# The out stage of the last three four-unit groups as seven block products, its halves placed in the next group's first step

## The chip, the cores and the metric

One core of one Trainium2 chip. The time is that of one execution on the device in microseconds (us); for the kernel before it is 228.29, the median of three runs (227.87 to 228.46). Engines: PE does matmuls (PEld is its weight loads), DVE, ACT and POOL work element by element, SP issues DMAs.

## The reference, cut to what matters

Attention with a decay, over blocks of 64 positions, and then a bilinear feed-forward layer on its output. The second part is what the change touches.

```
# q, k, v: (4, 8, 768, 64); per head, with powers of lam:
intra = (q_blk @ k_blk.T * Dmask) @ v_blk
out[blk] = intra + (q_blk * lam_pow) @ kv_state
kv_state = lam**64 * kv_state + (k_blk * rev_pow).T @ v_blk
# x = attention output, (3072, 512); w_a, w_b: (512, 1536); w_out: (1536, 512)
return ((x @ w_a) * (x @ w_b)) @ w_out
```

## The kernel before

The 3072 rows are 24 units of 128 positions, six for each batch entry. They go through the feed-forward layer in eight groups of 4, 1, 2, 4, 4, 4, 4 and 1 units (`GROUPS`, numbered from 0). While PE computes group g, the attention of later units is woven in: `PLAN[g]` lists (slot, piece, unit), and `hook(slot)` (L859) is called at fixed places of the group and emits the pieces of that slot. Nothing reorders them afterwards: each engine gets its instructions in the order in which the code emits them, PE, DVE, ACT, POOL and the DMA queue of SP alike. A piece of an early slot may so run far ahead of PE's place, if nothing ahead of it on its own engine waits.

Pieces: P scales k and q by powers of lam into `qk` (POOL, L318), makes `vb` of v, has SP transpose `qk` by DMA into `qkT` (L346), and asks for the loads of a unit two later (`pump`, L230). S is the scores (L374, 16 small matmuls) and their masks, a product with `lotri` on DVE (L391). V updates the running kv state (L438) and copies it (`KV_ENG` says by which engine). O forms the attention output of one or two units (L408) and ACT copies it into `xT` (L431). X forms three sums of `xT` for the next group on DVE (L620 to L622). C casts a part of w_out, WS forms one of eight sums of w_a and w_b (L206), W stores an early output.

Groups 3 to 6 (`Z_GROUPS`) run `ffn_z` (L625). Its first step computes x @ w_a and x @ w_b as seven products of blocks in place of eight (Strassen's way): six *pairs* n, each one chunk of 128 columns of both halves of d_ff. A product is four matmuls of 128x256. Of a pair, U (banks 0 and 1 in turn) takes products 1, 5, 3 and 2, V (banks 2 and 3 in turn) 4 and 6, W (bank 4) 0; ACT saves what stands in U and V in between (`snap`, L647: u1, v1, u2), DVE subtracts these from W (L679), U (L688) and V (L689). The last product 2 of a pair comes in the next pair (`finish`, L652): ACT copies U, and one DVE product makes `ab` of the pair's chunks (L658). Two slots a pair.

The second step, the *out stage* (L691 to L717), is plain: four tiles of 128 rows, each 12 matmuls of 128x512 with `ab` as weights and `wo_sb` streaming (L697), then an ACT copy (L552) and a store of 256 KB from SP's queue. Eight slots lie in it, and in it stand masks and X for the next group. Group 7 (one unit) runs `ffn` (L560): 12 times a and b of 128 columns with an ACT copy (L519) and a DVE product (L537), then 36 short matmuls (L557) and three copies and stores.

Eight 4 KB buffers (`wst`, L113) serve the weight loads, the snaps, `oab` and early outputs. Loads of q, k and v have four buffers each (L114); SP issues the four V loads of group 0 (L154) ahead of the first weight loads (L183).

Of the kernel before, what the change touches and what calls it, by code (L numbers as in the profile page):

```python
# [22 lines left out]
def _bc(ap, dims):  # L23
# [8 lines left out]
W_BUFS = 8  # L32
# [11 lines left out]
    0: [(0, 'V', 3), (8, 'C', 0), (9, 'C', 1), (15, 'C', 2), (18, 'C', 3), (23, 'PK', 4),  # L44
        (26, 'C', 4), (26, 'T', 4), (27, 'WS', 0), (28, 'WS', 1), (29, 'C', 5), (29, 'S', 4),
        (30, 'PV', 4), (31, 'WS', 2), (32, 'WS', 3), (33, 'O', 4), (34, 'WS', 4),
        (35, 'PK', 5), (35, 'PV', 5)],
    1: [(0, 'V', 4), (2, 'T', 5), (3, 'PK', 6), (4, 'WS', 5), (6, 'PV', 6), (6, 'S', 5),
        (7, 'T', 6), (8, 'WS', 6), (10, 'S', 6), (11, 'WS', 7), (12, 'O2', (5, 6)),
        (13, 'P', 7)],  # L50
    2: [(2, 'V', 6), (2, 'P', 8), (3, 'P', 9), (4, 'W', None), (5, 'V', 7), (5, 'PK', 10),
        (7, 'V', 8), (8, 'S', 7), (8, 'S', 8), (10, 'V', 9), (10, 'W', None), (11, 'PV', 10),
        (11, 'W', None), (12, 'P', 11), (12, 'W', None), (12, 'Q', (7, 8, 9, 10)),
        (13, 'P', 12), (14, 'O2', (9, 10)), (15, 'X', 3), (15, 'P', 13), (15, 'W', None)],
    3: [(0, 'S', 11), (2, 'P', 14), (4, 'S', 12), (7, 'S', 13), (7, 'P', 15),
        (9, 'O2', (11, 12)), (11, 'S', 14), (11, 'V', 13), (15, 'P', 16),
        (16, 'O2', (13, 14)), (16, 'X', 4), (17, 'P', 17), (17, 'P', 18), (17, 'S', 15),
        (19, 'S', 16), (19, 'P', 19)],
    4: [(3, 'V', 11), (3, 'V', 15), (4, 'S', 17), (5, 'O2', (15, 16)), (6, 'S', 18),
        (7, 'P', 20), (8, 'O2', (17, 18)), (9, 'V', 17), (9, 'P', 21), (11, 'S', 19),  # L60
        (13, 'S', 20), (14, 'X', 5), (19, 'V', 19), (19, 'P', 22)],
    5: [(4, 'S', 22), (5, 'S', 21), (8, 'O2', (19, 20)), (10, 'V', 21), (11, 'O2', (21, 22)),
        (11, 'P', 23), (16, 'X', 6)],
    6: [(0, 'S', 23), (11, 'O', 23)],
}
Z_GROUPS = (3, 4, 5, 6)
KV_ENG = dict(enumerate(["dve"] * 10 +
                        ["act"] * 2 +
                        ["dve"] +
                        ["act"] * 3 +  # L70
                        ["dve"] * 6 +
                        ["act"] +
                        ["dve"]))
VB_ENG = dict(enumerate(["pool"] * 7 +
                        ["dve"] * 3 +
                        ["act"] * 2 +
                        ["dve"] +
                        ["pool"] * 4 +
                        ["dve"] +
                        ["pool"] * 2 +  # L80
                        ["act"] +
                        ["dve"] +
                        ["pool"] * 2))
# [3 lines left out]
def kernel(  # L87
# [25 lines left out]
    wst_pool = ctx.enter_context(tc.tile_pool(name="wst", bufs=W_BUFS))  # L113
    ld_pool = ctx.enter_context(tc.tile_pool(name="ld", bufs=4))  # L114
    prep_pool = ctx.enter_context(tc.tile_pool(name="prep", bufs=6))
# [3 lines left out]
    a_pool = ctx.enter_context(tc.tile_pool(name="a", bufs=4))  # L119
# [5 lines left out]
    sum_pool = ctx.enter_context(tc.tile_pool(name="sum", bufs=1))  # L125
    ctx.enter_context(tc.manual_schedule())
# [36 lines left out]
    staged = {}  # L163
    w_off = [sum(W_CHUNKS[:i]) for i in range(len(W_CHUNKS) + 1)]
# [7 lines left out]
    def load_w(kind, c):  # L172
        t = wst_pool.tile([128, 1024], F32, name="wst", tag="wst")
        if kind == "o":
            t = t[:].rearrange("p (k n) -> p k n", k=2)
            nc.sync.dma_start(out=t, in_=wo_r[:, 2 * c:2 * c + 2, :])
        else:
            w = W_CHUNKS[c]
            t = t[:, :KS * w].rearrange("p (k n) -> p k n", k=KS)
            r = wa_r if kind == "a" else wb_r  # L180
            if c in W_HALVES:
                t = t.rearrange("p k n -> p (k n)").rearrange("p (k n) -> p k n", k=2)
            nc.sync.dma_start(out=t, in_=w_part(r, c))  # L183
        staged[kind, c] = t

    def cast_w(kind, c, eng):
        t = staged.pop((kind, c))
# [4 lines left out]
        if eng == "act":  # L192
            nc.scalar.copy(dst, t)
        elif eng == "first":
            nc.vector.tensor_copy(dst[:, :3, :128], t[:, :3, :128])
            nc.gpsimd.tensor_copy(dst[:, 3:, :128], t[:, 3:, :128])
            nc.gpsimd.tensor_copy(dst[:, :, 128:], t[:, :, 128:])
        else:
            nc.vector.tensor_copy(dst, t)  # L199
# [3 lines left out]
    wz = {kind: sum_pool.tile([128, 4, 2, HF], BF16, name="wz_" + kind, tag="wz_" + kind)  # L203
          for kind in "ab"}

    def weight_sum(i):  # L206
        kind, j = "ab"[i % 2], i // 2
        w, z = (wa_sb if kind == "a" else wb_sb), wz[kind]
        a11, a12 = w[:, 0:2, :HF], w[:, 2:4, :HF]
        a21, a22 = w[:, 0:2, HF:], w[:, 2:4, HF:]  # L210
        if j == 0:
            nc.vector.tensor_sub(z[:, 0], a22, a21)
        elif j == 1:
            nc.vector.tensor_sub(z[:, 1], a11, z[:, 0])
        elif j == 2:
            nc.vector.tensor_sub(z[:, 2], a12, z[:, 1])
        else:
            nc.vector.tensor_add(z[:, 3], a11, a21)
# [11 lines left out]
    def pump():  # L230
        while pending:
            kind, c = pending[0]
            if kind in "abo":
                if len(staged) >= W_BUFS:
# [9 lines left out]
    idle_sb = singles.tile([128, 512], BF16, name="idle_sb")  # L244
# [13 lines left out]
    for w, src in (("q", q), ("k", k)):  # L258
# [3 lines left out]
        for c in range(0, HP, n_c):  # L262
            t = wst_pool.tile([128, 1024], F32, name=w + "4", tag="wst")[:, :n_c * 512]
            t = t.rearrange("p (c b x) -> p c b x", c=n_c, b=2)
# [3 lines left out]
            staged[w + "4", c] = t  # L268
# [109 lines left out]
    def masks(u, kq):  # L378
        ms = mask(kq, split=False)
        U[u]["m"] = lambda i, hp: ms[i][:, hp, :]  # L380

    def mask(kq, split=False):
        ms = []
        for i in range(2):
            m = msk_pool.tile([128, HP, 128], BF16, name=f"m{i}", tag=f"m{i}")
            if split and i == 1:
# [97 lines left out]
    def pieces_O(us, nxt=()):  # L484
# [6 lines left out]
        for b in range(2):  # L491
            for u in us:
                intra(u, b)
            evac_o(us, b)
# [22 lines left out]
    def a_copy(ps, gt):  # L517
        a_sb = a_pool.tile([128, 512], BF16, name="a_sb", tag="a")
# [26 lines left out]
    def store(row, op, lo, hi, queue=None):  # L545
        if row < g_u0[KEEP_GROUPS]:
            o_sb = wst_pool.tile([128, 1024], F32, name="o_kept", tag="wst")[:, :d_model]
# [67 lines left out]
    def x_sums(g):  # L615
        xT = gx[g]
        z_add = sum_pool.tile([128, 2, 512], BF16, name="z_add", tag="z_add")
        z_sub = sum_pool.tile([128, KS, 256], BF16, name="z_sub", tag="z_sub")
        z_mix = sum_pool.tile([128, 2, 256], BF16, name="z_mix", tag="z_mix")
        nc.vector.tensor_sub(z_sub, xT[:, :, 0:256], xT[:, :, 256:512])  # L620
        nc.vector.tensor_add(z_add, xT[:, 0:2, :], xT[:, 2:4, :])
        nc.vector.tensor_add(z_mix, xT[:, 0:2, 0:256], xT[:, 2:4, 256:512])  # L622
        xz[g] = (z_add, z_sub, z_mix)

    def ffn_z(g, u0, xT, hook):  # L625
        z_add, z_sub, z_mix = xz.pop(g)
        ab = ab_pool.tile([128, FC, 512], BF16, name="ab", tag="ab")
        NP = FC // 2
# [16 lines left out]
        def snap(ps, tag):  # L645
            t = wst_pool.tile([128, 2, 256], F32, name=tag, tag="wst")
            nc.scalar.copy(t, ps)  # L647
            return t

        P = {}  # L650

        def finish(n):  # L652
            d = P.pop(n)
            product(d["U"], n, 2)
            oab = d["oab"]
            nc.scalar.copy(oab[:, 0], d["U"])  # L656
# [5 lines left out]
        def begin(n):  # L662
            d = P[n] = {}
            d["U"] = z_bank("U", n % 2)
            product(d["U"], n, 1, True)
            d["u1"] = snap(d["U"], "u1")

        for n in range(NP):
            if n != 1:
                begin(n)  # L670
            d = P[n]
            oab = d["oab"] = wst_pool.tile([128, 4, 2, 256], BF16, name="oab", tag="wst")
            d["V"] = z_bank("V", 2 + n % 2)
            product(d["V"], n, 4, True)
            v1 = snap(d["V"], "v1")
            hook(2 * n)
            W = z_bank("W", 4)
            product(W, n, 0, True)
            nc.vector.tensor_sub(oab[:, 2], W, d["u1"])  # L679
            product(d["U"], n, 5)  # L680
            u2 = snap(d["U"], "u2")
            if n:
                finish(n - 1)
            else:
                begin(1)
            product(d["V"], n, 6)
            product(d["U"], n, 3)
            nc.vector.tensor_sub(oab[:, 1], d["U"], v1)  # L688
            nc.vector.tensor_sub(oab[:, 3], d["V"], u2)  # L689
            hook(2 * n + 1)  # L690
# [4 lines left out]
        def out_part(t, fs):  # L695
# [7 lines left out]
        out_part(0, early[:3])  # L703
        finish(NP - 1)
        out_part(0, early[3:])
        hook(FC)
        out_part(1, early)
        hook(FC + 1)
        out_part(0, late)
        hook(FC + 2)  # L710
        out_part(1, late)
        hook(FC + 3)
        for t in (2, 3):
            out_part(t, early[:6])
            hook(FC + 2 * t)
            out_part(t, early[6:] + late)
            hook(FC + 2 * t + 1)  # L717
# [8 lines left out]
    scr = [ab_pool.tile([128, FC, 512], BF16, name="scratch", tag="ab") for _ in range(2)]  # L726
# [4 lines left out]
    def scale4(w, i, j):  # L731
# [5 lines left out]
        if w == "k" or j == 1:  # L737
            staged.pop((w + "4", c if w == "k" else 2 * i))
# [185 lines left out]
```

## Time and profile before

| | us |
|---|---|
| median of three runs | 228.29 (227.87 to 228.46) |
| the profiled execution | 228.72 |
| its span, first to last instruction | 227.0 |
| start, to b's first matmul in group 0 (L510) | 22.54 |
| group 4: pairs / out stage | 119.2 to 142.2 / to 153.0 |
| group 5: pairs / out stage | 153.0 to 174.4 / to 185.3 |
| group 6: pairs / out stage | 185.3 to 204.7 / to 215.6 |
| group 7 and the end | 215.6 to 227.0 |
| DVE / ACT / POOL busy | 154.6 / 117.0 / 59.2 |

How to read it: a row of the timeline has start, length, engine, line, operation, output<-inputs, sizes, count, and in brackets the idle time of that engine before it with what ended it. The length of one matmul holds its way through the array, so the pace of a stream is read from a run of equal ones, its length divided by their count. The chain of waits follows the end of the program back through whatever released each step; a piece has start, length and line. All times are us from the span's start unless ns is written.

### The profile page before, as it was taken

What the parts mean: (1) busy time and instruction counts of PE and PEld (TensorE: products, weight loads), DVE (VectorE), ACT (ScalarE), POOL (GpSimd) and SP (SyncE); (2) the same over time, 40 slices, a digit from 0 to 9 for tenths busy, and PEclk for the clock granted to TensorE, in tenths of its full rate; (3) what the DMA queues carried; (4) which work ended last, traced back from release to release, by engine and by line L of the source; (5) the groups of instructions that cost most, each with busy time, mean ns of one, the idle gap of its engine ahead of it and who ended that gap; (6) DMA issues with size and microseconds to landing.
All of it is one profiled execution on the core that took longest, in us unless ns stands there. A gap on an engine that the chain in (4) does not pass through costs nothing.

```text
span 227.0 us, 5349 instructions
## 1 busy us (share of the span) xinstructions
PE 217.8 (96%) x2127; PEld 148.3 (65%) x2127; DVE 154.6 (68%) x257; ACT 117.0 (52%) x233; POOL 59.2 (26%) x73
## 2 busy tenths in 40 slices
PE   7798999999899999999999999999999999999994
PEld 2374444447678758877458887448887458885493
DVE  0994773969959868999356988676988318773050
ACT  2685465037443267656247685127576236672261
POOL 6061000147843254424424434460000000000000
PEclk9999999999999999999999999999999999999999
DMA  4999999999999999999999999943020030000311
GB/s 131 318 261 350 359 387 319 271 222 196 233 192 200 240 187 269 212 233 184 181 247 237 205 186 231 169 153 92 3 48 1 27 144 18 1 3 0 141 46 46
DMA packets 97544, 39.40 MB, mean 174 GB/s; under 512 B 85488, under 2 KB 92016, under 8 KB 97520
## 3 DMA queue, kind: packets, MB, share of 16 engines
q1 hardware_dynamic: 97232, 39.00, 80.4%
q8 instruction: 16, 0.26, 0.5%
q10 hardware_dynamic: 288, 0.07, 0.1%
q14 instruction: 8, 0.07, 0.1%
HBM read 28.32 MB, written 6.29 MB: 152 GB/s over the span
## 4 chain that ended last, share of the span: by engine, by line
PE 77%; DMA 8%; SPq 6%; DVE 4%; issue 2%; ACT 1%; ACTq 0%; DVEq 0%
PE op L697 18%; PE U L641 15%; PE b_ps L510 9%; PE op L557 9%; PE a_ps L510 7%; PE V L641 7%; PE o_ps L408 4%; DMA wst<-in_moe_w_b_dram 4%; PE W L641 4%; SPq L154 3%; DMA qkT<-qk 3%; PE kq L374 2%; DMA q<-in_q_dram 2%; PE kvd L438 1%; SPq L183 1%
## 5 line engine op out<-in xcount | busy, mean ns | idle before, releaser
L697 PE MATMUL op<-wo_sb,ab 128*128 128x512 bf16 x192 | 43.3, 379 | 0.0
L391 DVE TENSOR_TENSOR m<-kq,lotri 128x512 bf16<-128x512 f32 x47 | 29.7, 681 | 13.7 <-PE kq L374 13.6
L647 ACT COPY u<-U 128x512 f32<-128x512 f32 x48 | 27.8, 587 | 18.7 <-PE U L641 17.9
L318 POOL TENSOR_TENSOR qk<-kf,lp_k 128x512 bf16<-128x512 f32 x18 | 19.7, 1096 | 53.2 <-DMA kf<-in_k_dram 51.0
L537 DVE TENSOR_TENSOR ab<-a_sb,b_ps 128x128 bf16<-128x128 bf16 (+2 forms) x48 | 19.3, 415 | 20.9 <-ACT a_sb L519 13.6
L697 PEld LDWEIGHTS <-ab 128*128 128x128 bf16 x192 | 18.2, 98 | 20.7
L318 POOL TENSOR_TENSOR qk<-qf,lp_q 128x512 bf16<-128x512 f32 x20 | 24.8, 1239 | 23.0 <-DMA qf<-in_q_dram 23.0
L510 PE MATMUL b_ps<-xT,wb_sb 128*128 128x128 bf16 (+2 forms) x192 | 27.6, 272 | 1.2 <-DVE wb_sb L199 1.0
L510 PE MATMUL a_ps<-xT,wa_sb 128*128 128x128 bf16 (+2 forms) x200 | 27.7, 268 | 0.0
L552 ACT COPY o_sb<-op 128x512 f32<-128x512 f32 (+2 forms) x21 | 11.1, 547 | 31.3 <-PE op L697 28.8
L658 DVE TENSOR_TENSOR ab<-oab 128x1024 bf16<-128x1024 bf16 x24 | 18.8, 783 | 9.1 <-ACT oab L656 9.0
L519 ACT CAST a_sb<-a_ps 128x128 bf16<-128x128 f32 (+2 forms) x48 | 17.2, 376 | 13.1 <-PE a_ps L510 11.5
L557 PE MATMUL op<-wo_sb,ab 128*128 128x512 bf16 (+2 forms) x120 | 22.5, 337 | 0.2 <-DVE ab L537 0.2
L510 PEld LDWEIGHTS <-wb_sb 128*128 128x128 bf16 x192 | 15.8, 98 | 7.7 <-DVE wb_sb L199 1.5
L641 PEld LDWEIGHTS <-wz_a 128*128 128x128 bf16 x192 | 18.3, 98 | 3.3 <-issue 0.3
L510 PEld LDWEIGHTS <-wa_sb 128*128 128x128 bf16 x200 | 16.0, 98 | 6.7 <-DVE wa_sb L199 0.4
L641 PEld LDWEIGHTS <-wz_b 128*128 128x128 bf16 x192 | 18.7, 97 | 2.2
L688 DVE TENSOR_TENSOR oab<-U,v 128x512 bf16<-128x512 f32 x24 | 16.4, 683 | 3.4 <-PE U L641 2.6
L641 PE MATMUL U<-xT,wz_a 128*128 128x256 bf16 x96 | 18.3, 272 | 0.0
L641 PE MATMUL U<-xT,wz_b 128*128 128x256 bf16 x96 | 18.3, 272 | 0.0
L679 DVE TENSOR_TENSOR oab<-W,u 128x512 bf16<-128x512 f32 x24 | 16.3, 681 | 0.9 <-PE W L641 0.9
L431 ACT CAST xT<-o_ps 128x512 bf16<-128x512 f32 (+1 forms) x24 | 12.2, 556 | 9.0 <-PE o_ps L408 8.9
(96 smaller groups left out, 337.0 us busy)
## 6 DMA issues: line engine op xcount, KB each, us to landing
vf<-in_v_dram SPq DMA_DIRECT2D x24, 256.0 KB, 5.0
qf<-in_q_dram SPq DMA_DIRECT2D x20, 256.0 KB, 5.1
kf<-in_k_dram SPq DMA_DIRECT2D x20, 256.0 KB, 5.4
out_dram<-o_sb SPq DMA_DIRECT2D x18, 256.0 KB, 2.2
wst<-in_moe_w_a_dram SPq DMA_DIRECT2D x6, 512.0 KB, 8.4
wst<-in_moe_w_b_dram SPq DMA_DIRECT2D x6, 512.0 KB, 9.0
wst<-in_moe_w_out_dram SPq DMA_DIRECT2D x6, 512.0 KB, 9.1
out_dram<-o_kept SPq DMA_DIRECT2D x5, 256.0 KB, 4.6
```

The costliest lines, as they stand in the source:

```text
L318: eng_of(eng).tensor_mul(dst.rearrange("p (c b) d -> p b c d", b=2), x[:].rearrange("p (b c) d -> p b c d", b=2), lp.rearrange("p (b c) o ...
L391: nc.vector.tensor_mul(m, kq[i], lotri_bc)
L510: nc.tensor.matmul(ps[:, lo:hi], lhsT=w_sb[:, s, f * 128:(f + 1) * 128], rhs=xT[:, s, lo:hi], start=(s == 0), stop=(s == KS - 1), skip_gro ...
L519: nc.scalar.copy(a_sb[:, :gt], ps[:, :gt])
L537: nc.vector.tensor_mul(ab[:, f, :gt], a_sb[:, :gt], ps[:, :gt])
L557: nc.tensor.matmul(op[:, lo:hi], lhsT=ab[:, f, t * 128:(t + 1) * 128], rhs=wo_sb[:, f, lo:hi], start=(f == 0), stop=(f == FC - 1))
L641: nc.tensor.matmul(ps[:, k, :], lhsT=wt[:, s, n * 128:(n + 1) * 128], rhs=rhs[i][:, s, :], start=(fresh and k == 0 and s == 0), stop=True, ...
L647: nc.scalar.copy(t, ps)
L658: nc.vector.tensor_mul(ab[:].rearrange("p (h i) (t c) -> p h i t c", h=2, t=2)[:, :, n], o5[:, :, :, 0, :], o5[:, :, :, 1, :])
L679: nc.vector.tensor_sub(oab[:, 2], W, d["u1"])
L688: nc.vector.tensor_sub(oab[:, 1], d["U"], v1)
L697: nc.tensor.matmul(ops[t][:].rearrange("p a b -> p (a b)"), lhsT=ab[:, f, t * 128:(t + 1) * 128], rhs=wo_sb[:, f, :], start=(f == 0), stop ...
```

## The change

The out stages of groups 4, 5 and 6 become seven products of blocks too: with ab split into four blocks (two halves of d_ff by two of 256 rows) and w_out into four (halves of d_ff by halves of its 512 columns). Three things are needed for it.

- Sums of w_out, once: five of 128x1536 (`out_sum`, piece WO, in group 3; POOL three, DVE two).
- Sums of ab for each of the three groups: eight of 128x768 (`ab_sum`, piece SM), 14 of the 24 on POOL, ten on DVE.
- The products as 14 *halves* (`out_half`, piece H), each six matmuls of 128x256 (three chunks, two row tiles). Two accumulators (banks 3 and 4); ACT saves three values and copies one out, DVE subtracts three; four stores of 256 KB, each of 256 columns of two row tiles.

The halves of group g are hooked into the pairs of group g+1 (those of group 6 between the 12 chunks of group 7). A pair has three slots now. In groups 5 and 6 ("joined") a pair has this order: U product 1, the last product of the pair before, slot 3n, V product 4, U product 5, slot 3n+1, V 6, U 3, slot 3n+2, W 0; V and W share bank 2. Groups 3 and 4 keep W in bank 4 and V in banks 2 and 3. Group 3 keeps the plain out stage.

With it the plan is drawn up anew. In group 4, P of 21 goes from slot 9 of the old two-slot pairs to slot 17, with 22, behind X of group 5, which POOL does, and an ab sum; P of 23 goes to slot 2 of group 5. S of 21, 22, 23 stand at slots 3, 6, 9 of group 5. Eleven masks go by an ACT copy (`raw_kq`) and a DVE product of it. Two WS, two C and three WO are POOL's. SBUF: the pool of eight is split into seven snaps of 2 KB, two `oab` and staging in tiles that are free early; q, k, v loads have three buffers each, `qk` and `vb` five.

```diff
+    4: [(0, 'V', 15), (1, 'S', 17), (2, 'P', 19), (4, 'O2', (15, 16)), (6, 'S', 18),
+        (9, 'P', 20), (10, 'O2', (17, 18)), (12, 'S', 19), (14, 'X', 5), (14, 'SM', (4, 0)),
+        (17, 'SM', (4, 2)), (17, 'S', 20), (17, 'SM', (4, 4)), (17, 'P', 21), (17, 'P', 22)],
+    5: [(0, 'SM', (4, 1)), (0, 'SM', (4, 3)), (1, 'H', (4, 0)), (1, 'V', 19),
+        (2, 'H', (4, 1)), (2, 'P', 23), (2, 'O2', (19, 20)), (3, 'S', 21), (4, 'H', (4, 2)),
...
-    ld_pool = ctx.enter_context(tc.tile_pool(name="ld", bufs=4))
-    prep_pool = ctx.enter_context(tc.tile_pool(name="prep", bufs=6))
+    ld_pool = ctx.enter_context(tc.tile_pool(name="ld", bufs=3))
+    prep_pool = ctx.enter_context(tc.tile_pool(name="prep", bufs=5))
...
+        p = (4, 0, 5, 6, 2)[i]
+        x, y = {4: (b11, b12), 0: (b11, b21), 5: (b11, b22), 6: (b12, b22), 2: (b21, b22)}[p]
+        eng = eng_of(WO_ENG[i])
+        (eng.tensor_sub if p in (2, 4) else eng.tensor_add)(wo_sums[p], x, y)
...
+            if i >= 2 - n_act:
+                raw_kq = raw_pool.tile([128, HP, 128], BF16, name="raw_kq", tag="raw")
+                nc.scalar.copy(raw_kq, kq[i])
+                nc.vector.tensor_mul(m, raw_kq, lotri_bc)
...
+            U = z_bank("U", pairs[0] % 2)
+            pairs[0] += 1
+            product(U, n, 1, True)
+            u1 = snap(U)
+            if joined:
+                if fin:
+                    fin.pop()()
+                hook(3 * n)
+            X = z_bank("V", 2 if joined else 2 + n % 2)
+            product(X, n, 4, True)
+            v1 = snap(X)
...
+            product(U, n, 5)
+            u2 = snap(U)
...
+            hook(3 * n + 1)
+            product(X, n, 6)
+            if joined:
+                nc.vector.tensor_sub(oab[:, 3], X, u2)
+            product(U, n, 3)
+            nc.vector.tensor_sub(oab[:, 1], U, v1)
...
+            hook(3 * n + 2)
+            if joined:
+                W = z_bank("W", 2)
+                product(W, n, 0, True)
+                nc.vector.tensor_sub(oab[:, 2], W, u1)
+            fin.append(lambda n=n, U=U, oab=oab: last_product(n, U, oab))
...
+    def ab_sum(g, i):
...
+        if j == 0:
+            eng.tensor_add(z3, a11, a21)
+        elif j == 1:
+            eng.tensor_sub(a21, a22, a21)
+        elif j == 2:
+            eng.tensor_sub(z1, a11, a21)
+        else:
+            eng.tensor_sub(z1, a12, z1)
...
+    O_ORDER = (4, 1, 5, 6, 3, 0, 2)
+
+    def out_half(g, i):
+        d = outs[g]
+        p, h = O_ORDER[i // 2], i % 2
...
+        c = "U" if p in (1, 5, 3, 2) else "V"
+        fresh = h == 0 and p in (4, 1, 0)
+        if fresh:
+            d[c] = z_bank("op", 3 if c == "U" else 4)
+        ps = d[c]
+        for n in range(h * NP // 2, (h + 1) * NP // 2):
+            for t in range(2):
+                nc.tensor.matmul(ps[:, t, :], lhsT=lhs[p][:, n, t * 128:(t + 1) * 128],
+                                 rhs=rhs[:, n, :], start=fresh, stop=True, skip_group_check=True)
+                fresh = False
+        if h:
+            if p in (4, 1, 5):
+                d[{4: "v1", 1: "u1", 5: "u2"}[p]] = snap(ps)
+            else:
+                o = o_pool.tile([128, 2, 256], F32, name="o_sb", tag="osb")
+                if p == 2:
+                    nc.scalar.copy(o, ps)
+                else:
+                    nc.vector.tensor_sub(o, ps, d[{6: "u2", 3: "v1", 0: "u1"}[p]])
...
+                nc.sync.dma_start(out=rows.rearrange("t p n -> p t n"), in_=o)
```

## The prediction

> **What bounds the kernel now.** First the page's busy shares, then the chain that ended last.
>
> ```profile
> PE 217.8 (96%) x2127; PEld 148.3 (65%) x2127; DVE 154.6 (68%) x257; ACT 117.0 (52%) x233; POOL 59.2 (26%) x73
> ...
> PE 77%; DMA 8%; SPq 6%; DVE 4%; issue 2%; ACT 1%; ACTq 0%; DVEq 0%
> PE op L697 18%; PE U L641 15%; PE b_ps L510 9%; PE op L557 9%; PE a_ps L510 7%; PE V L641 7%; PE o_ps L408 4%; DMA wst<-in_moe_w_b_dram 4%; PE W L641 4%; SPq L154 3%; DMA qkT<-qk 3%; PE kq L374 2%; DMA q<-in_q_dram 2%; PE kvd L438 1%; SPq L183 1%
> ```
>
> TensorE carries three quarters of the chain, and the largest single line is L697, the out stage that the change rewrites (192 matmuls, four groups). The stretches by stage say whether that stage is PE from end to end (columns: PE, weight loads, DVE, ACT, POOL busy, clock):
>
> ```profile
> 119.20:142.20 23.00, 22.78 (x267) 18.57 (x264) 19.82 (x32) 16.16 (x31) 10.21 (x11) 1.00 1.20 215
> 142.20:153.00 10.80, 10.78 (x61) 5.13 (x61) 7.39 (x9) 2.25 (x4) 5.64 (x6) 1.00 0.91 163
> 153.00:174.40 21.40, 21.40 (x269) 18.22 (x267) 17.91 (x29) 14.34 (x27) 0.00 (x0) 1.00 0.18 38
> 174.40:185.30 10.90, 10.90 (x56) 5.18 (x55) 2.94 (x6) 3.66 (x8) 0.00 (x0) 1.00 0.20 74
> ```
>
> These are the pairs of group 4, its out stage, the pairs of group 5, its out stage. PE is full at clock 1.00 in all; DVE is nearly as full beside the pairs and almost idle beside the out stages. So a PE microsecond removed is worth a microsecond, as long as what is put in its place does not wait.
>
> **The out stages.** Spacings come from the chain:
>
> ```profile
> 154.06 0.44 PE W L641 x4
> 154.50 0.87 PE U L641 x8
> ...
> 205.87 9.73 PE op L697 x45
> ```
>
> A 128x512 matmul takes 9.73/45 = 0.216 us, a 128x256 one 0.87/8 = 0.109. The old stage is 48 x 0.216 = 10.4 us; seven products of six chunks and two row tiles are 84 x 0.109 = 9.15. That is 1.23 us a group, **3.7 us** for three. The 84 weight loads are as many per column as in the pairs, which already run at that spacing, so they add nothing. The evictions (four ACT copies of 0.59 us a group) become four ACT copies and three DVE subtractions (0.68 each); four 256 KB stores stay four. All lie beside other PE work.
>
> **Sums.** Eight sums a group of 128x768 and five once of 128x1536. DVE's 128x1024 sum took 0.68 us undisturbed and its 128x1536 one 0.94, so 768 is about 0.52; POOL has only 512-element products (1.04, and 1.16 for the one mask), so I take 1.55 for 768, 2.05 for 1024 and 3.1 for 1536. Ten of the 24 go to DVE, 14 to POOL; three of the five weight sums, two old weight sums, two casts and all of group 5's x sums go to POOL too. DVE has 3.5 us free beside group 5's pairs and 5 beside group 6's, and the stages grow by 9 us each: the total fits, order decides.
>
> **Two engines on one memory.** While POOL scaled unit 21, DVE's product took twice its time:
>
> ```profile
> 137.25 1.05 POOL L318 TENSOR_TENSOR qk<-kf,lp_k 128x512 bf16<-128x512 f32 x1 [4.37 <-DMA kf<-in_k_dram]
> 137.48 1.35 DVE L658 TENSOR_TENSOR ab<-oab 128x1024 bf16<-128x1024 bf16 x1 [0.69 <-ACT oab L656]
> 138.25 1.49 POOL L318 TENSOR_TENSOR qk<-qf,lp_q 128x512 bf16<-128x512 f32 x1
> 138.76 0.68 DVE L688 TENSOR_TENSOR oab<-U,v 128x512 bf16<-128x512 f32 x1
> ```
>
> 1.35 for 0.68, then POOL's 1.49 for 1.04, a meeting costing each side some 0.45 to 0.67; the subtraction from PSUM kept its 0.68. I use these meetings.
>
> [...]
>
> **A joined pair (groups 5 and 6).** V and W share one bank now. With 0 at the end of the last W: U1 to 0.44, the last pair's U to 0.88, V to 1.31, U to 1.75, a half (6 x 0.109 = 0.65) to 2.4, V to 2.84, U to 3.28, a half to 3.93, W to 4.37. Three waits are tight. The next V waits for DVE's subtraction of W: 0.06 + 0.68 + 0.05 = 0.79 against 0.88, 0.09 of slack, gone when DVE takes a half's output just before. W waits for the subtraction of V, 2.9 to 3.6 against 3.93. DVE's product (ACT copy 1.0 to 1.6, product 1.65 to 2.3) must be done before that: a delay d puts W at 3.03 + d, so 0.9 costs nothing and 1.6 costs 0.7. Where units 19/20 and 21/22 put their O work, ACT is about 0.7 us behind and the next u1 costs some 0.1. I take 0.8 for the twelve pairs, from 0 to 3 (0.25 a pair).
>
> **Unit 21.** Its scaling moves from slot 9 of group 4 to slot 17, on POOL behind group 5's three x sums and one ab sum, and its scores stay early in group 5. Count from group 4's start (119.2 before). PE reaches the end of O(17,18)'s matmuls after 3.28 (pair 0: six products, V, S), 4.20 (seven and O), 3.50 (seven and S), five products 2.19 and 0.80: 14.0; ACT has xT at 15.1. POOL: 2.05 + 2.05 + 1.05, ab sum 1.55, to 21.8; two or three meetings with DVE make 22.9; two scales 2.1, so 25.0 (the load, asked for after unit 19, has landed by then: at 137.25 in this trace). Then SP's transpose: landing took 3.0 to 6.1, median 4.8, 3.9 for the two on an idle DMA. PE wants it at slot 3: group 4's pairs end at 22.1, group 5's first pair with two halves, V 19 and O(19,20) takes 5.7, two U products 0.88: 28.7. With 3.9 the wait is 0.3, with 4.8 it is 1.2; I take **0.7**, from 0 to 2.7 (4.8, two more meetings and 0.6 for slower sums). All of PE's list stands behind it. Units 22 and 23 leave POOL at 28 and, after 23's load, at 33.6, 1 to 3 us before their scores; later ab sums have about 1 us.
>
> DVE's third ab sum waits for that POOL sum (22.9) in front of group 4's last product and group 5's first subtractions; unit 20's masks hold DVE to 23.4 anyway. Beside the x sums, DVE's products of the last two pairs may be held up for most of 2.05 us; then the subtraction of U, which the next pair's last product waits for, is late: **0.4**, from 0 to 1.3.
>
> **The start.** The load tiles of q, k and v go from four buffers to three, so SP's fourth V load waits for POOL's cast of the first.
>
> ```profile
> 10.68 1.05 SPq L154
> 11.72 0.04 issue
> 11.77 1.14 SPq L183
> ```
>
> That cast ran 12.11 to 12.72, so this issue moves from 10.68 to 12.75 and the weight loads behind it by up to 1 us; b's first chunk, at 21.76, is what PE then waits for. DMA is full from 6 us on (share 0.97 or more in each 2 us), and the V loads ahead land until 14.5, so the queue should stay fed: **0.2**, from 0 to 1.0. It can't gain.
>
> **Groups 0 to 3.** Casts, weight sums and masks move between engines (eleven masks become an ACT copy and a DVE product of SBUF, 0.59 and 0.4 for 0.68), all beside a full PE. In group 1 PE now waits 0.49, 0.61 and 0.15 us on DVE (k scale, ab); two weight sums leave DVE there, but one of 3.1 us now sits on POOL ahead of unit 6's scales: 50.5 + 3.1, then two scales of 1.04, or 1.70 and 1.49 as here, to 55.7 or 56.8. T of unit 6 wants them at slot 5: 52.1 + 0.2 + six chunks of 0.45 + V + T = 55.7. So 1.25 becomes 0 to 1.1, or more if DVE's sums bunch: **-0.4**, from -1.2 to +0.9. The 0.32 for unit 13's transpose should go, as its scores move a third of a pair back, and 0.18 at group 4's end: **-0.3**, -0.5 to 0. POOL's other new sums lie before unit 19 (scales end about 128.6, scores at 135) and cost nothing; without that cover, 1 to 3.
>
> **The end.** Group 6's halves run between group 7's chunks, all PE work; the same 36 matmuls close. The last copy reuses the tile of the last half's store: copy 0.65 and landing 2.2 make 2.9, PE needs 3.1: **0.1**, 0 to 0.7.
>
> **Sum**, against the profiled execution's 228.72 (span 227.0 and 1.7 around it): -3.7 + 0.8 + 0.7 + 0.4 + 0.2 - 0.4 - 0.3 + 0.1 = -2.2, so 226.5. The median shown is 0.43 lower, 228.29: **226.1**.
>
> **Rivals.**
> 1. *Nothing waits.* The terms for pairs, unit 21 and group 4 are 0: another 1.9 us, **224.2**. For it: a slack of some tenths in every walk. Against: DVE and POOL already disturb each other.
> 2. *POOL becomes the bound (slower).* The place is the scores of unit 21 and what queues behind. If the six POOL instructions of that walk all take 1.43 times as long (1.49/1.04), their 8.8 us become 12.6, 2.7 more than with my meetings; unit 21 waits 3.4, group 4's end 0.9, the pairs 1.5: 226.1 + 2.7 + 0.5 + 0.7 = **230.0**. It decides once these three terms, 1.9 in my sum, pass 4.1. Against: most DVE work there reads PSUM, and the rows above show that unharmed.
> 3. *The pairs take it back (no change).* One bank for V and W costs 0.25 in each of twelve pairs, 3.0 instead of 0.8: **228.3**.
> 4. *It does not do what it says*, halves slower than 0.109: excluded by the pairs' own spacing but for a few per cent.
>
> **How the numbers follow.** A run of this kernel can tell 0.3% (0.7 us). Forecast 0.53 (224.9 to 227.5), rival 1 0.17, rival 3 0.10, rival 2 0.20. Faster: 0.53 + 0.17 = 0.70; same 0.10; slower 0.20. The range takes in most of rival 1, rival 3 and the lower half of rival 2: 223.9 to 229.5, leaving out about 0.05 below and 0.12 above. Faster cases alone: 223.9 to 227.5.
>
> **What would show it.** Halves x6 at 0.65 us in the chain; PE's waits listing scores of unit 21 on a transpose (0 to 2.7); V on DVE's subtraction of W in joined pairs (under 0.1 each); DVE's product at 1 to 2 us where POOL runs; b's first chunk within 1 us of 21.8; group 7 gapless. Wrong if PE shows waits on POOL's ab sums, or if the start slips by over 1 us.

## The result, and the profile after

The changed kernel takes 236.25 us, median of four runs (235.89 to 237.09), beside 228.38 for the kernel before in the same runs (227.87 to 228.53). The ratio is 1.0354, 95% interval 1.032 to 1.0388: slower by some 8 us, where 2.2 us faster was forecast and 229.5 was the upper end of the range. The profiled execution took 237.09, its span is 235.4 (before 228.72 and 227.0).

From the page after: the busy shares, and the chain that ended last, by engine and by line.

```profile
PE 218.2 (93%) x2235; PEld 159.9 (68%) x2235; DVE 170.4 (72%) x266; ACT 123.8 (53%) x247; POOL 112.6 (48%) x101
...
PE 59%; DVE 10%; ACT 3%; issue 3%; POOL 1%; ACTq 0%; DVEq 0%
```

PE's share of the chain fell from 77% to 59% and DVE's rose from 4% to 10%: PE now waits, and for DVE. POOL is busy for 112.6 in place of 59.2 but has 1% of the chain; what it does to the others the chain doesn't show as POOL's.

By stage, in us of the profiled executions. The old out stage of a group is 48 x 0.217 = 10.4 and 84 matmuls of a half's kind are 9.15, so each stage can be compared without them:

| stage | before | after | difference | forecast |
|---|---|---|---|---|
| start to a's first matmul (L510, L587) | 17.75 | 19.35 | +1.6 | +0.2 |
| groups 0 to 3 | 101.5 | 103.4 | +1.9 | -0.7 |
| groups 4 to 6, without out stages or halves | 65.0 | 72.9 | +7.9 | +1.9 |
| three out stages, as plain or as halves | 31.2 | 27.5 | -3.7 | -3.7 |
| group 7 to PE's end, without halves | 8.4 | 8.9 | +0.5 | 0 |
| after PE's end | 3.2 | 3.4 | +0.2 | +0.1 |

Of the 1.9 in groups 0 to 3, 1.7 (half of 3.4) is PE's clock, which stood at 0.50 from 19.5 to 22.9 in this execution (below); in the other three the mean clock is 0.998 to 1.0, so most of that part is in this one only. The other 0.2 hides more. Before, PE waited for b's first chunk in group 0, and the later start took that wait over (first line before, second after):

```profile
22.54 1.04 PE L510 MATMUL b_ps<-xT,wb_sb 128*128 128x512 bf16 x4 [0.98 <-DVE wb_sb L199]
24.50 1.67 PE L587 MATMUL b_ps<-xT,wb_sb 128*128 128x512 bf16 x7
```

Counted from this matmul to group 4, the changed kernel takes 98.24 (to 122.74) in place of 96.70 (to 119.24): 1.5 more, at full clock.

The view by windows divides groups 4 to 6 (columns: PE, weight loads, DVE, ACT, POOL busy, clock, DMA):

```profile
122.74:147.26 24.52, 22.65 (x269) 18.39 (x268) 22.40 (x33) 17.27 (x33) 15.48 (x10) 1.00 0.90 181
147.26:163.31 16.05, 11.42 (x138) 9.08 (x135) 14.41 (x17) 8.31 (x17) 12.78 (x11) 1.00 0.53 99
163.31:184.96 21.65, 21.04 (x233) 18.01 (x231) 15.95 (x25) 12.49 (x25) 10.71 (x6) 1.00 0.11 37
184.96:213.97 29.01, 29.01 (x274) 25.32 (x272) 19.55 (x32) 15.55 (x30) 8.58 (x6) 1.00 0.12 38
```

The last line is group 6, with joined pairs and group 5's halves: PE busy for all of its 29.01 us. Before, group 6 took 30.26 with its plain stage; 30.26 - 10.4 + 14 x 0.655 = 29.0. There the change does what it was forecast to do, to the tenth. The loss lies in group 4 and in the first 16 us of group 5 (second line), where DVE and POOL are both nearly full and PE is busy for 11.42 of 16.05. PE's waits after name DVE's subtractions (us in total, times, longest):

```profile
PE U L722 <- DVE oab L761: 3.4, 5, 1.6
PE W L722 <- DVE oab L759: 2.3, 2, 1.6
PE a_ps L587 <- DVE wa_sb L247: 1.4, 1, 1.4
...
PE op L844 <- DVE ab L730: 1.2, 1, 1.2
```

Those subtractions read PSUM and took their usual 0.68. The rows ahead of them on DVE did not. Timeline of the changed kernel at the seam of groups 4 and 5, POOL, DVE and PE in order of start:

```profile
140.91 2.12 POOL L698 TENSOR_TENSOR z_add<-xT 128x1024 bf16<-128x1024 bf16 x1
141.11 2.20 DVE L460 TENSOR_TENSOR m<-raw_kq,lotri 128x512 bf16<-128x512 bf16 x1
...
143.97 0.38 PE L722 MATMUL W<-z_add,wa_sb 128*128 128x256 bf16 x2 [0.55 <-DVE oab L751]
...
146.62 1.63 POOL L819 TENSOR_TENSOR ab<-ab 128x768 bf16<-128x768 bf16 x1 [2.29 <-DVE zab L817]
147.06 1.74 DVE L730 TENSOR_TENSOR ab<-oab 128x1024 bf16<-128x1024 bf16 x1
...
149.45 0.38 PE L722 MATMUL U<-z_sub,wa_sb 128*128 128x256 bf16 x2 [1.58 <-DVE oab L761]
```

A mask of 0.43 us takes 2.20 and ends at 143.31, 0.28 after POOL's sum ended at 143.03. An ab product of 0.68 takes 1.74 and ends at 148.80, 0.55 after POOL's 148.25. The same two remainders, 0.28 for 512 elements and 0.54 to 0.56 for 1024, stand in five more rows (masks at 126.02 and 160.24; products at 143.84, 152.77 and 158.33): in all seven DVE's row ends this long after POOL's, though they began 0.09 to 1.33 us after POOL's start. All of PE's waits over 0.5 us between 128 and 163 follow such rows. In the changed kernel's list of waits none of PE's or DVE's is put down to POOL: what is late is DVE's instruction, not a result of POOL's.

### The profile page after: what moved, and what is told of

It reads as the page before. It is cut to its first block, busy times and chain, and to the rows that moved or that the text cites. A ratio compares the mean times of both kernels' runs of the same rounds, so it can differ in the third digit from the quotient of the medians.

```text
span 235.4 us, 5620 instructions
## 1 busy us (share of the span) xinstructions
PE 218.2 (93%) x2235; PEld 159.9 (68%) x2235; DVE 170.4 (72%) x266; ACT 123.8 (53%) x247; POOL 112.6 (48%) x101
## 4 chain that ended last, share of the span: by engine, by line
PE 59%; DVE 10%; ACT 3%; issue 3%; POOL 1%; ACTq 0%; DVEq 0%
PE U L722 14%; PE op L844 10%; PE V L722 7%; PE op L634 5%; PE op L784 5%; PE W L722 4%; PE b_ps L587 4%; PE a_ps L587 4%; DVE ab L730 4%; PE o_ps L485 3%; PE kq L445 2%; DVE m L468 1%; DVE oab L761 1%; PE kvd L515 1%; ACT oab L728 1%
## 5 line engine op out<-in xcount | busy, mean ns | idle before, releaser
L614 DVE TENSOR_TENSOR ab<-a_sb,b_ps 128x128 bf16<-128x128 bf16 (+2 forms) x48 | 19.5, 418 | 20.9 <-PE b_ps L587 12.2
L389 POOL TENSOR_TENSOR qk<-kf,lp_k 128x512 bf16<-128x512 f32 x18 | 21.9, 1219 | 25.5 <-DMA kf<-in_k_dram 20.5
L587 PE MATMUL a_ps<-xT,wa_sb 128*128 128x128 bf16 (+2 forms) x200 | 29.3, 280 | 2.2 <-DVE wa_sb L247 1.4
L730 DVE TENSOR_TENSOR ab<-oab 128x1024 bf16<-128x1024 bf16 x24 | 21.7, 906 | 12.2 <-ACT oab L728 12.0
L587 PE MATMUL b_ps<-xT,wb_sb 128*128 128x128 bf16 (+2 forms) x192 | 27.5, 272 | 0.6 <-ACT oab L728 0.5
L389 POOL TENSOR_TENSOR qk<-qf,lp_q 128x512 bf16<-128x512 f32 x20 | 23.7, 1187 | 1.0 <-DMA qf<-in_q_dram 1.0
L587 PEld LDWEIGHTS <-wa_sb 128*128 128x128 bf16 x200 | 17.5, 101 | 9.3 <-DVE wa_sb L247 1.6
L468 DVE TENSOR_TENSOR m<-kq,lotri 128x512 bf16<-128x512 f32 x36 | 23.2, 682 | 0.5 <-PE kq L445 0.3
L722 PEld LDWEIGHTS <-wz_a 128*128 128x128 bf16 x192 | 18.3, 98 | 3.5 <-issue 0.3
L587 PEld LDWEIGHTS <-wb_sb 128*128 128x128 bf16 x192 | 15.7, 98 | 7.2 <-issue 0.8
L722 PEld LDWEIGHTS <-wa_sb 128*128 128x128 bf16 x144 | 13.2, 97 | 10.5 <-issue 7.8
L722 PE MATMUL U<-xT,wz_b 128*128 128x256 bf16 x96 | 18.3, 272 | 0.0
L722 PE MATMUL U<-xT,wz_a 128*128 128x256 bf16 x96 | 18.3, 272 | 0.0
L728 ACT CAST oab<-U 128x512 bf16<-128x512 f32 x24 | 14.2, 591 | 6.0 <-PE U L722 6.0
L408 POOL CAST vb<-vf 128x512 bf16<-128x512 f32 x17 | 11.6, 680 | 11.1 <-DMA vf<-in_v_dram 11.1
L761 DVE TENSOR_TENSOR oab<-U,u 128x512 bf16<-128x512 f32 x24 | 16.3, 680 | 0.0
L634 PEld LDWEIGHTS <-ab 128*128 128x128 bf16 x120 | 10.3, 98 | 8.5
```

Of the source, the lines that this page charges most:

```text
L389: eng_of(eng).tensor_mul(dst.rearrange("p (c b) d -> p b c d", b=2), x[:].rearrange("p (b c) d -> p b c d", b=2), lp.rearrange("p (b c) o ...
L468: nc.vector.tensor_mul(m, kq[i], lotri_bc)
L587: nc.tensor.matmul(ps[:, lo:hi], lhsT=w_sb[:, s, f * 128:(f + 1) * 128], rhs=xT[:, s, lo:hi], start=(s == 0), stop=(s == KS - 1), skip_gro ...
L614: nc.vector.tensor_mul(ab[:, f, :gt], a_sb[:, :gt], ps[:, :gt])
L634: nc.tensor.matmul(op[:, lo:hi], lhsT=ab[:, f, t * 128:(t + 1) * 128], rhs=wo_sb[:, f, lo:hi], start=(f == 0), stop=(f == FC - 1))
L722: nc.tensor.matmul(ps[:, k, :], lhsT=wt[:, s, n * 128:(n + 1) * 128], rhs=rhs[i][:, s, :], start=(fresh and k == 0 and s == 0), stop=True, ...
```

## The experiments

Theory A: a DVE instruction that takes its operands from SBUF waits for the whole POOL instruction that it meets; PE then waits for what is queued behind it on DVE. Theory B: POOL's work is late, and the two engines only share a rate. Theory C: the joined pairs, with V and W in one bank, cost by themselves. Times are given as the ratio to the kernel before in the same call, with its interval; 0.01 is 2.3 us. The changed kernel stands at 1.0354.

**The held instructions, from DVE's side.** The eleven masks read PSUM again:

```diff
+MASK_ACT = {u: 0 for u in range(24)}
```

> Edit: the eleven masks that go by an ACT copy and a DVE product of two SBUF operands are DVE products of the PSUM scores again (0.68 us in place of 0.43). Theory A (a DVE instruction whose operands are all in SBUF waits for the whole POOL instruction that it meets): the rows of L460 with 2.05, 2.20 and 1.82 us go, and with them most of PE's waits of 0.79 at 128.7, 0.55 and 0.53 at 144.0 and 145.5, and 1.65 at 162.7: 2 to 3.5 us off the 236.25. Theory B (POOL's sums are simply late, and DVE only shares the memory's rate): within 0.7 us, as POOL's list is the same and DVE has 0.25 more in each mask. Theory C (the joined pairs' one bank): within 0.7 us.

Measured 1.0227 (1.017 to 1.0285), 2.9 us less than the changed kernel. The waits of 0.79, 0.55 and 0.53 are gone and 1.65 became 0.98; 1.58 and 1.24, which ab products caused, stayed. Each mask is 0.25 us longer on DVE, and the kernel is faster: A, not B or C. The edit also takes eleven copies off ACT, but in groups 4 to 6 of the changed kernel PE waited for ACT only once, for 0.16.

**From POOL's side.** The same sums in pieces of 256 elements, on the same engine:

```diff
+    def piecewise(eng, op, dst, x, y, ax):
...
+        for i in range(dst.shape[ax]):
+            at = (slice(None),) * ax + (slice(i, i + 1),)
+            getattr(nc.gpsimd, op)(dst[at], x[at], y[at])
...
-        eng_of(XS_ENG[g, 0]).tensor_sub(z_sub, xT[:, :, 0:256], xT[:, :, 256:512])
...
+        piecewise(XS_ENG[g, 0], "tensor_sub", z_sub[:], xT[:, :, 0:256], xT[:, :, 256:512], 1)
```

> Edit: POOL's sums of x, ab and w_out are cut into instructions of 256 elements (4 for 1, 3 for 1, 6 for 1); nothing moves between engines. Theory A (whole instruction): a DVE product that meets one waits 0.6 us at most in place of 1.6 to 3.1, and 2 to 4 us go, unless POOL's own extra instructions (about 60 at some 0.05 to 0.1) make its sums late. Theory B (the two share a rate): DVE's long rows stay long, and the time stays or rises by up to 2 us.

Measured 1.0182 (1.0118 to 1.0246), 3.9 us less, though POOL is busy 10.9 us longer (123.5): 256 elements take 0.64 to 0.68, where a third of 1.64 is 0.55. A again; under B more POOL work could not help.

**The sums on DVE.**

> Edit: all sums of x, ab and w_out on DVE (14 of 0.55, 5 of 0.42 to 0.69 and 3 of 1.24 us more there: 14.5 us), POOL keeps scales, casts and the two weight sums. Theory A: the meetings with sums go, those with scales (1.0 us each) stay; DVE is fuller, but it had been held about 14 us by meetings: 2 to 4 us off. If DVE's own list is the bound: same or slower by up to 3 us. Theory C: PE's waits for V and W in joined pairs stay and grow.

Measured 1.0521 (1.0435 to 1.0606): the forecast of A was wrong. POOL's sums fell away, and PE now waits, in the profiled execution (the slowest of the four, 245.06), for DVE's own ab sums (1.95, 1.92 and 0.98 us) and a mask (1.38). Its longest wait, 3.32, still stands behind two held rows, as the x sums now meet POOL's scales:

```profile
144.23 1.58 POOL L392 TENSOR_TENSOR qk<-kf,lp_k 128x512 bf16<-128x512 f32 x1 [2.03 <-DMA kf<-in_k_dram]
144.83 1.53 DVE L701 TENSOR_TENSOR z_add<-xT 128x1024 bf16<-128x1024 bf16 x1
145.77 1.49 POOL L392 TENSOR_TENSOR qk<-qf,lp_q 128x512 bf16<-128x512 f32 x1
146.28 1.26 DVE L702 TENSOR_TENSOR z_mix<-xT 128x512 bf16<-128x512 bf16 x1
149.86 0.59 PE L725 MATMUL U<-z_sub,wa_sb 128*128 128x256 bf16 x2 [3.32 <-DVE oab L764]
```

So the run doesn't speak against A; but DVE has no room for 14.5 us more where the sums stand, and POOL can't simply be relieved by it.

**The start.**

```diff
...
+        if (w, u) == ("v", 3):
+            t = snap_pool.tile([128, 512], F32, name="vf3", tag="snap")
...
```

> Edit: the fourth V load of group 0 goes to a free 2 KB tile instead of waiting for the cast of the first. If this wait is what makes the start late (a's first chunk, cast at 18.86 in place of 17.27, PE idle 1.44 us and then at half clock from 20 to 23): a's first matmul returns to about 17.8, b's wait of 1.0 us comes back, and 1 to 2.5 us go (the clock's part, 1.5 us, only in those runs that had it). If the weights' new staging or the DMA queue is what is late, the time stays within 0.5.

Measured 1.0289 (1.0228 to 1.035), 1.5 us less, but the interval overlaps that of the changed kernel (1.032 to 1.0388), so the size stays open. SP issued the weights at 11.78 in place of 13.25 (before 11.77) and a's first matmul came at 18.05 in place of 19.35. In the changed kernel the rows of SP, and then DVE's, were:

```profile
5.67 7.48 SPq L193 DMA_DIRECT2D vf<-in_v_dram  x4
13.25 1.08 SPq L232 DMA_DIRECT2D wst<-in_moe_w_a_dram  x2
```

```profile
18.86 0.42 DVE L247 CAST wa_sb<-wst 128x384 bf16<-128x384 f32 x1 [1.68 <-DMA wst<-in_moe_w_a_dram]
```

Before, this cast ran from 17.27 to 17.70, and PE came free just then: a's chunk had no cover at all against an issue that is 1.5 later.

**The mechanism alone, in the kernel before.** POOL did nothing in groups 5 and 6 before the change. Two kernels add one idle sum (POOL, 128x1024 bf16, read by nobody) to each of their twelve pairs, once whole and once in four pieces:

```diff
             nc.vector.tensor_sub(oab[:, 2], W, d["u1"])
+            if g in (5, 6):
+                extra_sum(oab[:, 2])
```

> The kernel before, with nothing changed but one idle POOL sum of 128x1024 bf16 (2.1 us) in each of the twelve pairs of groups 5 and 6, released by DVE's subtraction of W; its result is read by nobody. In groups 5 and 6 POOL did nothing before. Theory A (whole instruction): where POOL begins first, DVE's ab product takes up to 2 us and ends 0.3 to 0.6 after POOL's end; the subtractions behind it are late, PE waits for DVE in most pairs, and the time rises by 4 to 9 us. Theory B (shared rate): both some tenths longer, 0 to 2 us. Theory C: nothing.

> The same sums in the kernel before, each as four instructions of 128x256. Theory A: DVE's product can slip in between two pieces, so it is held by some 0.6 us at most each time: at most half of what the whole sums cost. Theory B: the same bytes, so the same or more than the whole ones. Theory C: nothing.

Measured 1.016 (1.0094 to 1.0227) whole and 1.001 (0.9978 to 1.0042) in pieces: 3.7 us against nothing that can be measured, for the same sums. One pair of each, first whole (one span for two POOL sums), then in pieces:

```profile
192.39 4.88 POOL L628 TENSOR_TENSOR extra<-oab,wa_sb 128x1024 bf16<-128x1024 bf16 x2 [0.59 <-DVE oab L685]
...
195.49 2.33 DVE L664 TENSOR_TENSOR ab<-oab 128x1024 bf16<-128x1024 bf16 x1 [0.60 <-ACT oab L662]
197.74 0.68 DVE L696 TENSOR_TENSOR oab<-U,v 128x512 bf16<-128x512 f32 x1
...
198.47 0.38 PE L647 MATMUL U<-z_sub,wa_sb 128*128 128x256 bf16 x2 [1.02 <-DVE oab L696]
```

```profile
193.14 1.17 DVE L665 TENSOR_TENSOR ab<-oab 128x1024 bf16<-128x1024 bf16 x1 [0.62 <-ACT oab L663]
194.23 0.68 DVE L697 TENSOR_TENSOR oab<-U,v 128x512 bf16<-128x512 f32 x1
```

POOL's span ends at 197.27, DVE's product at 197.82: 0.55 after, as in the changed kernel. The next subtraction is late and PE waits 1.02. Only four of the twelve products met a sum long enough (waits of 0.65, 0.82, 1.02 and 0.97, 3.5 us in all); the measured 3.7, just under the 4 to 9 expected, is these four. This is the least that theory A needs, with no change of plan, bank or buffer beside it.

**How much is the holding?** The first mends together, and then with P of unit 21 moved:

> The three edits together: masks from PSUM, POOL's sums in pieces of 256, the fourth V load in a tile of its own. Alone they took about 2.9, 3.9 and 1.5 us (by their ratios to the kernel before, 1.0227, 1.0182, 1.0289, against 1.0354). Theory A (whole instruction): the first two cure partly the same meetings, so 5 to 7 us together: 229 to 231. If they cure different things: 228. What is left should be PE waits on DVE's ab product where it meets POOL's scales (1.0 us each).

> As the three mends together, and P of unit 21 right after group 5's x sums, where POOL had been idle for 2.3 us, in place of behind the second ab sum. Theory A: its two scales no longer meet DVE's products of group 4's last pairs, and the halves' wait of 1.2 to 1.5 us on the last ab product goes: 1 us less than the three mends. If PE waits there because DVE's list is full: no change.

Measured 1.0187 (1.012 to 1.0253) and 1.0198 (1.0154 to 1.0242). The three mends don't add up, as masks from PSUM and pieces cure partly the same meetings; together they are no better than pieces alone (1.0182), and the 229 to 231 expected was missed by 1.4 us. Moving unit 21 gave nothing: its scales met another product (1.52 us at 143.09). Two kernels left parts of the change out:

> The out stages of groups 4, 5 and 6 plain again, without sums of ab and w_out; plan, engines, masks and buffers otherwise as in the changed kernel. It prices what comes with the change beside its products. Theory A: PE has 3.7 us more to do, the meetings with ab and w_out sums go (1.65 at 162.7, most of 1.58 at 149.4, 0.79 at 128.7), those with group 5's x sums and the scales stay: 230 to 233. If the loss lies in the products and their joined pairs alone (theory C): 228 to 229.5, before plus the late start.

> Leaves out all 24 sums of ab (the three products that read them take a block of ab in their place), so the output is not the reference's; also masks from PSUM, x sums on DVE, the fourth V load apart. The 252 matmuls of the halves, the joined pairs and the evictions stay: the price of the change without its meetings. Theory A: 224.5 to 227, with only scales and casts to meet. Theory C (the joined pairs' bank and order cost by themselves) or halves dearer than 0.109: 229 or more.

The plain out stage with the rest of the change took 1.0318 (1.0286 to 1.0351), above the 233 expected: the new plan puts masks and x sums beside the pairs, and without halves between these, PE waits there for ACT (1.1 us) and DVE (1.2) and the long cover of the plain stage lies unused. By its profile 2.5 us of the loss lie ahead of group 4 and 4.2 in groups 4 to 6, where the waits that the list names come to 2.7; so it is no clean price of the rest, and a part of it stays unexplained. Leaving out the sums of ab took 1.023 (1.0153 to 1.0306), far above the 224.5 to 227 expected from A. Its DVE rows show why:

```profile
142.22 1.53 DVE L703 TENSOR_TENSOR z_sub<-xT 128x1024 bf16<-128x1024 bf16 x1
143.68 1.53 DVE L704 TENSOR_TENSOR z_add<-xT 128x1024 bf16<-128x1024 bf16 x1
```

That kernel's x sums were on DVE, and two scales of POOL (142.16 to 144.65) held both of them, 1.53 for 0.69. PE then waited 2.86, up to 147.39, and its clock after it was 0.50 from 148.5 to 151.7 and 0.64 on average from 147.3 to 152.0, which makes some 3.4 us at half, an estimate from these two. So it was open whether DVE's list at the seam, which before lay beside the old out stage, is a cause by itself. Two kernels changed the order there:

```diff
-        (17, 'SM', (4, 2)), (17, 'S', 20), (17, 'SM', (4, 4)), (17, 'P', 21), (17, 'P', 22)],
-    5: [(0, 'SM', (4, 1)), (0, 'SM', (4, 3)), (1, 'H', (4, 0)), (1, 'V', 19),
+        (17, 'SM', (4, 2)), (17, 'S', 20), (17, 'P', 21)],
+    5: [(0, 'SM', (4, 1)), (0, 'SM', (4, 3)), (0, 'P', 22), (0, 'SM', (4, 4)), (1, 'H', (4, 0)), (1, 'V', 19),
```

> The changed kernel with the order at the seam alone: unit 22's scales and one ab sum of DVE behind the last ab product of group 4. If holding is the whole cause: the product no longer meets unit 22's scales, 1.2 us of wait at 154.4 go, other meetings may come: 0 to 1.5 us off. If DVE's list is a cause by itself: 1 to 2 us off.

> The three mends together, and at the seam of groups 4 and 5 the scales of unit 22 and one ab sum of DVE behind the last ab product in place of ahead of it. Theory A with DVE's list as what is left: the halves' wait of 1.5 us at 149.8 falls to under 0.5, others stay: 1 to 1.5 us less than the three mends (230.5 to 231.5). If unit 22 is then too late: its scores wait for a transpose, no gain.

Alone it took 1.0263 (1.0222 to 1.0304), 2.1 us less than the changed kernel and a little more than either forecast; with the three mends 1.0096 (1.0058 to 1.0134), 231.4 us, the best form that was run of the change with its whole result. In both the halves' wait on the last product (1.24 and 1.51) is gone, and a wait of 0.9 for DVE's subtraction of V came a little later. An order that helps fits both causes: it takes work out of DVE's list and a product out of unit 22's way. The run that tells them apart leaves DVE's list and takes POOL away:

> POOL does nothing from group 4's second half on: units 20 to 23 use unit 19's scaled q and k (and its vb where POOL made it), group 5 uses group 4's x sums (group 6 two of them), POOL's sums of ab and w_out are left out and a block of ab or w_out takes their place, so the output is not the reference's. DVE's, ACT's and PE's lists stay as in the changed kernel, but for x sums never theirs; one ab sum reads another operand. If holding by POOL is the whole loss of groups 4 and 5 (some 8 us there against the forecast): those two groups lose under 1 us and the time falls by 6.5 to 8 us, to 228.5 to 230 (the late start stays). If DVE's list at the seam, without the old out stage's cover, is a cause by itself: 2 to 4 us of waits stay at 143 to 155, and the time is 231 to 233.

Measured 1.0071 (1.0025 to 1.0118), 6.5 us less than the changed kernel. Groups 4 to 6 of its profile, from one end to the other:

```profile
121.39:205.10 83.71, 83.21 (x905) 70.91 (x904) 63.45 (x105) 53.23 (x105) 2.22 (x2) 1.00 0.48 94
```

PE is busy for 83.21 of 83.71. The kernel before, with 18.3 for the halves in place of 31.2, would be 96.18 - 31.2 + 18.3 = 83.3. The run also takes away every wait for a result of POOL's, but the changed kernel's list has none. So the holding by POOL is the loss of groups 4 to 6, all but 0.4 of 7.9; DVE's list at the seam and the joined pairs are not causes by themselves. With POOL silent the kernel still isn't faster than before: up to group 4 it is 2.2 us late (121.39 in place of 119.24; a's first matmul at 18.91, b's at 22.53 on time again, so the loss is behind that), and 0.5 more go at group 7's beginning. The profiled execution is its fastest, 228.21; why the median is 1.2 above it isn't shown.

**Pieces once more.**

> The replanned kernel, with POOL's scales of q and k cut in two, its two weight sums in pieces of 256, the output of units 5 and 6 one slot earlier in group 1, and the scores of units 7 and 8 two slots earlier in group 2. Theory A (the length of POOL's instructions is what DVE waits for): the rows of ab products beside scales fall from 0.8 to 1.4 us towards 0.7 to 0.9, PE's 0.81 and 0.95 at 144.0 and 149.8 shrink; with PE's waits of 0.46 at 64.5 and 0.52 at 77.6 gone, 1 to 2.5 us less than the replanned kernel: 1.000 to 1.005 of the kernel before. If what is left is DVE's full list: no more than the 1 us of groups 1 and 2.

> Masks from PSUM, the fourth V load apart, and the order at the seam, with POOL's sums whole. Against the replanned kernel with pieces (1.0096 of before) it tells what the pieces are still worth once the masks read PSUM. Holding by whole instructions: 1 to 3 us slower than with pieces (ab products still meet x and ab sums). If the pieces' own length (POOL 20 to 70% longer) costs as much as they free: the same or faster.

Cutting everything took 1.0147 (1.0094 to 1.0201), not the 1.000 to 1.005 expected. The held rows did shrink (products beside scales 0.8 to 1.1), but a weight sum that takes 3.09 whole took

```profile
49.80 5.24 POOL L275 TENSOR_TENSOR wz_a<-wa_sb,wz_a 128x256 bf16<-128x256 bf16 x6
```

and behind it unit 6's scales were late: PE waited 1.39 us for POOL at 57.4, and 0.87 for a transpose at 158.3. The replanned kernel with whole sums took 1.0147 (1.0114 to 1.0181); against 1.0096 with pieces the intervals overlap, so what pieces are worth there, 0 to 2 us, stays open.

## Why the prediction was wrong, by its own steps

- **The out stages, -3.7: right.** Group 6 shows it (29.01 against 29.0). That halves are dearer than 0.109 is excluded, as said.
- **The joined pairs, 0.8: too much.** In group 6 and with POOL silent, PE waits 0.15 at most for what shares the bank. The W waits of 1.65 and 0.61 stand in joined pairs, but each follows a held row. Rival 3 falls.
- **Unit 21, 0.7: no wait.** In the changed kernel PE nowhere waits for a transpose of units 21 to 23; PE itself was late by then, so the walk's own slack wasn't tested.
- **Two engines on one memory: the step that failed.** "A meeting costing each side some 0.45 to 0.67" was read from partners of 1.04 us and then used for partners of 1.6 to 3.1. In the rows the price of a meeting goes with what was left of POOL's instruction: 1.06 of 1.19 left (a product beside an ab sum), 1.77 of 1.92 (a mask beside an x sum), 1.62 of 1.77 (a mask beside a sum of w_out). My own rows had the mark: the product of 1.35 ended at 138.83, 0.53 after POOL's 138.30, and I read it as a fixed price. The 0.4 for group 4's end is the only term that lets products be held by a whole sum. No run shows it by itself: before, no ab product lost more than the 0.67 at 137.48, and after, beside group 5's x sums, a product lost 0.36 (1.04 at 143.84) and a mask 1.77 (141.11). Nearly all of the 7.9 is of that kind, where my three terms for groups 4 to 6 came to 1.9. The number of meetings was wrong too: I took it for protection that "most DVE work there reads PSUM". It is true, but a held product held the PSUM work queued behind it (the product of 1.74 at 147.06, then PE's 1.58 at 149.45), and the masks that the change moves to an ACT copy are new victims, with both operands in SBUF; alone they cost 2.9 us. In all, PE lost 6.95 us of the 7.9 in seven waits, three of them in group 4, four in group 5 and none in group 6.
- **The start, 0.2: 1.6 at a's first matmul.** I named b's first chunk, at 21.76, as what PE would wait for; it was a's first chunk, whose cast ended at 17.70 before, just as PE came free. The row was in the profile and I did not walk it. b's chunk was cast at 21.83 (before 21.79), so the old wait of 0.98 for it covers a part: with masks from PSUM, where the clock stayed full, a came at 19.58 and b at 23.21, 0.7 later than before.
- **Groups 0 to 3, -0.7: some +1.5** from b's first matmul on, at full clock; the sign was wrong. Group 1's three waits of 1.25 us shrank to 0.2 and unit 13's 0.32 is gone, but 0.46 at group 2's first matmul (on ACT's xT), 0.52 at 79.8 (on DVE's st) and two for DVE's subtractions (0.18 and 0.28) came with the new plan. The named waits so come to 1.6 in both kernels, and where the 1.5 lies isn't shown.
- **The end, 0.1:** 0.5 at group 7's beginning (b's chunk on ACT's copy) and 0.2 behind PE.
- **Rival 2** had the engine right and the path wrong: it let POOL be late for unit 21's scores, and priced 230.0. No wait is put down to POOL's results; it was in the way.

Two more things stay open. The replanned kernel's executions lie from 229.3 to 231.8 at full clock, and no profile here says why. And what the rest of the change costs without halves isn't priced cleanly by the plain out stage.

## What to carry to other kernels

Before work is moved from DVE to an idle POOL, list DVE's instructions that take SBUF operands beside it: those that met a long POOL instruction here ended 0.28 us (512 elements) or 0.54 to 0.56 (1024) after it, up to 2.20 us long in place of 0.43, and what was queued behind them was late (PE waited up to 1.65). Price a meeting by the length of POOL's instruction (up to 1.77 us beside a sum of 2.12 here), not by one meeting seen elsewhere, and look for the mark in a trace: a DVE row that is too long and ends a fixed time (here 0.28 or 0.55) after a POOL row. Short POOL instructions, or a PSUM operand for DVE, lessened it (3.9 and 2.9 us of some 8 here), at the price of longer lists: POOL was busy 10.9 us longer, and DVE 0.25 in each mask.

## What the runs showed of the hardware

- One-operand casts are held too: DVE's cast of a 128x512 f32 tile of SBUF took 1.26 in place of 0.42 and ended 0.28 after POOL's scale (151.59 to 152.85; POOL's end 152.57).
- POOL's bf16 sums of SBUF took 0.64 to 0.68 for 256 elements, 1.64 for 768, 2.13 for 1024 and 3.09 for 1536 when undisturbed. POOL is held in turn: an ab sum of 768 took 2.11 in place of 1.64 beside DVE's product (175.49).
- After a wait PE's clock stood at 0.50 for some 3.4 us. In the changed kernel it followed the wait of 1.44 at the start:

```profile
19.50:22.90 3.40, 3.40 (x17) 2.29 (x16) 1.77 (x3) 0.64 (x2) 0.37 (x1) 0.50 1.09 360
```

  It costs 1.7 us here, an estimate: half of these 3.40. Without the sums of ab it followed the wait of 2.86 (0.50 from 148.5 to 151.7, as above). Not each wait brings it: after 1.63 us of wait at the same place, with masks from PSUM, the clock stayed at 1.00 (19.60 to 23.00). What decides it no run here shows.
